# Sending each head's scores in two transfers, by two queues, with four banks for the first mixing

## The chip, the cores and the metric

The kernel runs on one core of a Trainium2 chip. The metric is device time of one execution in microseconds (us); the median of several executions is given for a kernel. Differences of about 1% are what a measurement of this kernel can tell from none. The engines are TensorE (PE in the rows; PEld is its loading of weights), VectorE (DVE), ScalarE (ACT), GpSimd (POOL) and SyncE (SP), which here only issues transfers.

## The reference

The reference is attention whose heads are mixed before and after the softmax, and then two layers of matrix products on its output. Only the attention is touched by the change.

```python
# q, k, v: (4 batches, 12 heads, 448 rows, 64); w_pre, w_post: (12, 12)
scores = scale * np.matmul(q, k.transpose(0, 1, 3, 2))
scores = np.einsum('bhij,hg->bgij', scores, w_pre)
scores = scores - np.max(scores, axis=-1, keepdims=True)
attn = np.exp(scores)
attn = attn / (np.sum(attn, axis=-1, keepdims=True) + 1e-09)
attn = np.einsum('bhij,hg->bgij', attn, w_post)
x = np.matmul(attn, v)                 # heads side by side: (1792, 768)
h = x @ w_in                           # (1792, 2048)
x = (h * np.cos(h)) @ w_out            # (1792, 768)
h = np.maximum(np.maximum(x @ w1, x @ w2), x @ w3)
return h @ w_out2
```

## The kernel before, in words

**Blocks, slots and visits.** The 448 score rows of a batch are cut into four blocks of 10, 12, 12 and 11 slots; a slot is ten rows (`RI`), so a block has 100 to 120 rows. There are 16 blocks, numbered through all batches. For a block, `qk` (L552) multiplies two heads at a time: four matmuls for each of the six pairs of heads, into a bank of PSUM for each head (pool `ps_x`, two banks). `evac` copies a head's scores to SBUF (tile `s`, on ScalarE or VectorE; the copy is recorded at L460), and `send` (L566) moves them by a transfer from SBUF to SBUF into the tile of slots, `t`. There a slot's ten rows of all twelve heads lie side by side on 120 partitions, so that heads can be mixed by a matmul. There are two tiles `t`, used by even and odd blocks in turn.

**A visit** takes two slots. `mix1` (L575) mixes the heads of both into two banks of the pool `ps_m` (half `a` of the rows in each), `rowmax` (L583, VectorE) and `soft` (L589, ScalarE, exp with the row sums) make the softmax of each bank into a tile `e`, the three small operations `guard` (L594), `recip` (L598) and `wscale` (L603) on VectorE make the second mixing's weights with the row sums in them (`w2s`), `mix2` (L616) mixes the heads again, which also transposes, into a bank of the pool `ps_t` for each slot, and `keep` copies the two banks to the tile `a2`. A batch has 23 visits.

**The product with v.** Two neighbouring blocks are one entry of `HALVES`; when all of its visits are kept, `av` (L640) multiplies by v in three pieces of two pairs of heads, each piece into two banks of `ps_t`, `keepx` copies them to `xs` (L460 again), and `out` (L655) sends them to DRAM (`xT`). Below, Q stands for the four matmuls of one `qk`, M for a visit's first mixing, X for its second, and A for a piece of `av`; Q6.5 is the last pair of heads of block 6, M6:0 the first visit of block 6, A3/1 the second piece of the fourth entry of `HALVES`.

**The layers behind.** xT is loaded a batch at a time into a place of the tiles `t` (`x<-xT`, L139) and cut in two parts; the weights are loaded (`wraw`), converted on ScalarE and VectorE, and the products run as matmuls at L156 to L158.

**What sets the order.** A planner (`Plan`) knows each operation's rank, what it comes after, the places that it takes and frees, and a duration for each engine that may do it, written in the code by hand (letters T, V, A, P and D for TensorE, VectorE, ScalarE, GpSimd and SyncE's queue). It picks one operation after another, and the engine for those that may run on two. Each engine then runs its own list in that fixed order, and waits where data are late. SP's transfers also run on eight semaphores in turn, so the ninth waits for the first to land.

## Time and profile before

| | |
|---|---|
| median of three runs | 1171.14 us (1169.19 to 1177.53) |
| the profiled execution's own time | 1172.04 us |
| its span from first to last instruction | 1170.3 us |
| TensorE busy | 1130.7 us, 97% of the span |
| VectorE busy | 992.9 us, 85% |
| ScalarE busy | 656.3 us, 56% |
| GpSimd busy | 79.8 us, 7% |

The shares are means over two stages. In the attention the matmuls are short and alternate between four kinds of work; in the layers behind they run without a gap. The profile gives a line's instructions in groups, the waits by who ended them, and the chain of work that ended last, in order of time.

### The profile page before, as it was taken

Reading aid. Unit: us, or ns where it says so; the run is one execution under the profiler, and the core shown is the slowest. Engines: PE = TensorE matmul, PEld = TensorE weight load, DVE = VectorE, ACT = ScalarE, POOL = GpSimd, SP = SyncE. Lnnn points to the kernel's source line nnn. Section 1 sums busy time; section 2 is a strip of 40 time slices with the busy share of each in tenths; the row PEclk is TensorE's granted clock in tenths of the full one; section 3 lists DMA queues with packets and bytes.
Section 4 is the critical chain, followed back from the end, with each engine's and each line's share of the span. In section 5 each row is a group of like instructions: output and inputs, shape, how many; then the busy total and the mean of one; then the engine's idle time right before and its main releaser. Section 6 shows DMA issues by size and latency. Waiting matters only on the chain.

```text
span 1170.3 us, 29431 instructions
## 1 busy us (share of the span) xinstructions
PE 1130.7 (97%) x11836; PEld 926.5 (79%) x11836; DVE 992.9 (85%) x2083; ACT 656.3 (56%) x1468; POOL 79.8 (7%) x69
## 2 busy tenths in 40 slices
PE   7899999899898899999999999999999999999998
PEld 2566566565556699999999999999999999999987
DVE  5878777777778899999999999997788679778994
ACT  3656556655657687555555555555534354445472
POOL 4000000000005110000000000000001021011110
PEclk9999999999999999999999999999999999999999
DMA  6785565645553655343434344431002221222233
GB/s 220 226 242 163 169 195 158 185 132 153 155 170 116 213 155 149 115 136 115 135 115 135 115 135 121 130 108 34 1 28 82 61 67 35 76 66 69 82 117 113
DMA packets 90696, 146.02 MB, mean 125 GB/s; under 512 B 8928, under 2 KB 73536, under 8 KB 90560
## 3 DMA queue, kind: packets, MB, share of 16 engines
q1 hardware_dynamic: 90304, 144.12, 40.8%
q8 instruction: 93, 1.52, 0.5%
q14 instruction: 43, 0.35, 0.1%
q0 software_dynamic: 256, 0.02, 0.0%
HBM read 84.96 MB, written 20.45 MB: 90 GB/s over the span
## 4 chain that ended last, share of the span: by engine, by line
PE 84%; DMA 6%; DVE 5%; issue 1%; ACT 1%; SPq 1%; ACTq 0%; DVEq 0%
PE ps L156 21%; PE ps L158 21%; PE ps L157 21%; PE mps L575 6%; PE aps L640 5%; PE aps L616 5%; PE ps L552 4%; DMA t<-s 3%; DMA x<-xT 1%; DVE nm L583 1%; DMA v<-in_v_dram 1%; DVE s L460 1%; DMA wraw<-in_w_in_dram 0%; ACT e L589 0%; DVE a L460 0%
## 5 line engine op out<-in xcount | busy, mean ns | idle before, releaser
L158 PE MATMUL ps<-x,w 128*128 128x448 f32 x816 | 300.0, 368 | 2.4 <-DVE x L147 1.5
L156 PE MATMUL ps<-x,w 128*128 128x448 f32 x816 | 300.4, 368 | 0.8 <-ACT gh L857 0.6
L157 PE MATMUL ps<-x,w 128*128 128x448 f32 x816 | 299.8, 367 | 0.5 <-DVE w L296 0.3
L156 PEld LDWEIGHTS ps<-x,w 128*128 128x128 f32 x816 | 153.7, 188 | 17.6 <-issue 2.4
L158 PEld LDWEIGHTS ps<-x,w 128*128 128x128 f32 x816 | 153.6, 188 | 17.4 <-POOL x L147 2.0
L157 PEld LDWEIGHTS ps<-x,w 128*128 128x128 f32 x816 | 153.7, 188 | 14.8 <-POOL w L131 0.8
L589 ACT ACTIVATE e<-mps,nm 128x448 f32<-128x448 f32 (+1 forms) x184 | 116.9, 637 | 79.2 <-DVE nm L583 59.3
L616 PEld LDWEIGHTS aps<-w2s,e 60*64 60x64 f32 x5760 | 108.7, 136 | 51.2 <-issue 23.8
L156 PE MATMUL ps<-gh,w 128*128 128x448 f32 x384 | 140.9, 367 | 0.0
L157 PE MATMUL ps<-gh,w 128*128 128x448 f32 x384 | 140.7, 366 | 0.0
L158 PE MATMUL ps<-gl,w 128*128 128x448 f32 x384 | 140.4, 366 | 0.0
L583 DVE TENSOR_REDUCE nm<-mps 128x1 f32<-128x448 f32 (+1 forms) x184 | 110.2, 616 | 30.8 <-PE mps L575 29.3
L293 ACT CAST w<-wf 128x384 fp32r<-128x384 f32 x168 | 81.1, 514 | 74.5 <-DVE wf L285 54.2
L616 PE MATMUL aps<-w2s,e 60*64 60x60 f32 x5760 | 112.7, 220 | 8.9 <-DVE w2s L603 6.2
L575 PE MATMUL mps<-t,w 64*64 64x448 f32 (+1 forms) x720 | 106.4, 558 | 10.2 <-DMA t<-s 6.2
L552 PE MATMUL ps<-k,q 64*64 64x448 f32 (+3 forms) x736 | 99.0, 551 | 5.1 <-ACT s L460 2.5
L814 DVE TENSOR_TENSOR acc<-ps,acc 128x448 f32<-128x448 f32 x168 | 100.2, 615 | 1.4 <-PE ps L158 1.4
L252 ACT ACTIVATE wf<-wraw 128x384 f32<-128x384 f32 x112 | 61.9, 553 | 51.3 <-DMA wraw<-in_w_out_dram 37.7
L296 DVE TENSOR_TENSOR w<-wf,w 128x384 fp32r<-128x384 f32 x132 | 73.7, 579 | 19.1 <-ACT w L293 18.3
L296 POOL TENSOR_TENSOR w<-wf,w 128x384 fp32r<-128x384 f32 x36 | 42.1, 1177 | 684.6 <-DVE wt L256 371.8
L640 PE MATMUL aps<-a,v 128*64 128x220 f32 (+1 forms) x768 | 78.0, 356 | 4.7 <-ACT xs L460 3.2
L640 PEld LDWEIGHTS aps<-a,v 128*64 128x64 f32 x768 | 54.2, 136 | 34.2 <-issue 5.9
(121 smaller groups left out, 1736.7 us busy)
## 6 DMA issues: line engine op xcount, KB each, us to landing
t<-s SPq DMA_DIRECT2D x96, 210.0 KB
wf<-w SPq DMA_DIRECT2D x96, 192.0 KB
wraw<-in_w_out_dram SPq DMA_DIRECT2D x44, 384.0 KB
wraw<-in_w_dram SPq DMA_DIRECT2D x36, 384.0 KB
wraw<-in_w_in_dram SPq DMA_DIRECT2D x32, 384.0 KB
t<-s SPq DMA_DIRECT2D x48, 192.5 KB
w<-wf SPq DMA_DIRECT2D x48, 192.0 KB
t<-s SPq DMA_DIRECT2D x43, 175.0 KB
```

The source lines that it names most:

```text
L156: mm(w[0], x[0], start=first, stop=False)
L157: mm(w[1], x[0], start=False, stop=False)
L158: mm(w[0], x[1], start=False, stop=last)
L293: return nc.scalar.copy(A[x][0], w())
L296: return eng.tensor_sub(A[x][1], w(), f32(A[x][0]))
L552: nc.tensor.matmul(live["s", n, 2 * hp + g][r:end], live["q", b, hp][half, i0 + r:i0 + end], live["k", b, hp][half], start=True, stop=True)
L575: nc.tensor.matmul(live["m", v, a][64 * y:64 * y + 64], w1[k], grids[n % 2][k, t + y, :], start=True, stop=True)
L583: nc.vector.tensor_reduce(nm, of(v, live["m", v, a]), axis=AX.X, op=ALU.max, negate=True)
L589: nc.scalar.activation(of(v, e), of(v, live["m", v, a]), AF.Exp, bias=live["nm", v, a], scale=1.0, accum_out=live["z", v][:, a:a + 1])
L616: nc.tensor.matmul(live["a", v, y][64 * c:64 * c + 64, j, :, a, :], live["e", v, a][k, o:o + 64], live["w2s", v][k, a], start=True, stop=True)
L640: nc.tensor.matmul(ps[64 * g:64 * g + 64, :m], vt[:, j, g, :], a2[:, j, 2 * hp + g, :m], start=j == 0, stop=j == JB - 1)
L814: return nc.vector.tensor_add(acc, po, acc) if fg else nc.scalar.copy(acc, po)
```

## The change

Four things change together.

- **Sends.** A head's scores of a block go in two transfers, one for slots 0 to 5 and one for the rest, and each is issued by SP or by GpSimd, as the planner finds. Each half of the tile `t` is a place of its own in the plan (`t0`, `t1`): a visit waits for the half that holds its slots, and a half is free once its visits are mixed. `keepx` copies in two parts for each block, since the rows are now spread over the slots of each half.
- **Banks.** `ps_m` has four banks instead of three and `ps_t` two instead of three; `av` puts both pairs of heads of a piece into one bank. `s` has seven tiles instead of eight, `e` six instead of five.
- **Blocks.** The first batch's first two blocks and the last batch's last two are entries of `HALVES` of their own, so there are ten entries and 30 pieces of `av` instead of 8 and 24. The last batch's blocks are in the order 12, 11, 12, 10.
- **The planner's numbers.** Durations and the times until a result can be used are written anew, and a piece of `av` stands behind a certain visit.

```diff
-HALVES = [[[10, 12], [12, 11]]] * B
+HALVES = [[[10], [12], [12, 11]], [[10, 12], [12, 11]], [[10, 12], [12, 11]], [[12, 11], [12], [10]]]
...
+HALF = 6
+BUFS = {"k": 10, "q": 9, "s": 7, "e": 6, "w2s": 3, "v": 7, "xs": 6, "a2": 2, "ps_m": 4, "ps_t": 2, "ps_x": 2}
...
-    def send(n, h, eng):
+    def send(n, h, y, eng):
         slots = score[n][3]
-        queue_of[eng].dma_start(grids[n % 2][PAD + h:PAD + RI * H:H, :slots, :], live.pop(("s", n, h))[:RI * slots])
+        start, end = y * HALF, min(slots, (y + 1) * HALF)
+        queue_of[eng].dma_start(grids[n % 2][PAD + h:PAD + RI * H:H, start:end, :],
+                                live["s", n, h][RI * start:RI * end])
...
-        for hp in pairs(x):
-            vt = live["v", b, hp]
-            live["av", hp] = ps_t.tile([128, JB, H, RI], F32, name="aps")
-            ps = live["av", hp] = live["av", hp].rearrange("p j g i -> p (j g i)")
+        both = ps_t.tile([128, JB * H * RI], F32, name="aps")
+        for n, hp in enumerate(pairs(x)):
+            ps = live["av", hp] = both[:, n * NHALF:(n + 1) * NHALF]
             for j in range(JB):
                 for g in range(2):
-                    nc.tensor.matmul(ps[64 * g:64 * g + 64, :m], vt[:, j, g, :], a2[:, j, 2 * hp + g, :m],
+                    nc.tensor.matmul(ps[64 * g:64 * g + 64, :m], live["v", b, hp][:, j, g, :], a2[:, j, 2 * hp + g, :m],
                                      start=j == 0, stop=j == JB - 1)
...
-            copy(eng, xs[:, o:o + m].rearrange("p (r t) -> p r t", t=slots),
-                 ps[:, c:c + m].rearrange("p (t r) -> p r t", r=RI))
+            for t in range(0, slots, HALF):
+                part, w = RI * t, min(HALF, slots - t)
+                copy(eng, xs[:, o + part:o + part + RI * w].rearrange("p (r t) -> p r t", t=w),
+                     ps[:, c + part:c + part + RI * w].rearrange("p (t r) -> p r t", r=RI))
...
-                add(evac, (n, h), r, {"A": 0.55, "V": 0.62}, [("qk", n, hp)], turn=True, takes=[place := copy_place(n, h)[0]], frees=[(ring, ("qk", n, hp), h % 2)])
-                if h == 0:
-                    plan.add(("new_t", n), r, lambda _: None, {}, [("evac", n, 0)], takes=["t"])
-                add(send, (n, h), r, {"D": score[n][2] / 118.0}, [("evac", n, h), ("new_t", n)], turn=True, frees=[(place, ("evac", n, h))], lands=2.5)
+                add(evac, (n, h), r, {"A": 0.42, "V": 0.53}, [("qk", n, hp)], turn=True, lands=0.16, takes=[place := copy_place(n, h)[0]], frees=[(ring, ("qk", n, hp), h % 2)])
+                for y in range(2):
+                    if h == 0:
+                        plan.add(("new_t", n, y), r, lambda _: None, {}, [("evac", n, 0)], takes=[f"t{y}"])
+                    add(send, (n, h, y), r + 0.2 * y, {"D": 0.78, "P": 0.78}, [("evac", n, h), ("new_t", n, y)],
+                        behind=[("send", n, h - 1, y)] if h else [], frees=[(place, ("evac", n, h))], lands=3.5)
...
-        add(mix1, (y,), i, {"T": 0.8}, [("wmix", 0), ("fill", n % 2)] + [("send", n, h) for h in range(H)], turn=True, takes=["ps_m"] * 2,
-            frees=[("t", ("new_t", n))])
+        add(mix1, (y,), i, {"T": 0.78}, [("wmix", 0), ("fill", n % 2)] + [("send", n, h, t // HALF) for h in range(H)], turn=True, takes=["ps_m"] * 2,
+            frees=[(f"t{t // HALF}", ("new_t", n, t // HALF))])
...
-        add(mix2, (y,), i + 1.5, {"T": 0.05 + 0.45 * len(slots)}, [key("wscale")], turn=True, takes=["ps_t"] * len(slots),
+        add(mix2, (y,), i + 1.5, {"T": 0.04 + 0.465 * len(slots)}, [key("wscale")], turn=True, takes=["ps_t"] * len(slots),
...
+    def from_visit(y):
+        return [("mix1", y)] if 0 <= y < len(visits) else []
...
+        room = min(12, starts[halves[half + 1][4][-1] + 1] - 1 - ylast) if half + 1 < len(halves) else 12
...
-            add(av, (half, x), r, {"T": 3.25}, [("vget", b, hp) for hp in pairs(x)] + ends, turn=True, takes=["ps_t"] * 2,
-                frees=[("a2", start)] + [("v", ("vget", b, hp)) for hp in pairs(x) if half % 2])
+            add(av, (half, x), r, {"T": 0.2 + 0.0139 * halves[half][3]}, [("vget", b, hp) for hp in pairs(x)] + ends, turn=True, takes=["ps_t"],
+                frees=[("a2", start)] + [("v", ("vget", b, hp)) for hp in pairs(x) if halves[half][1] + halves[half][2] == S],
+                behind=from_visit(ylast + 2 + x * room // 3))
...
-        add(xget, (n,), r, {"D": 3.6}, [("out", 2 * n + x, hp) for x in range(2) for hp in range(H // 2)] + [("xget", 0)] * n
-            + [("block", FG)], takes=["t"])
+        add(xget, (n,), r, {"D": 3.6}, [("out", x, hp) for x, y in enumerate(halves) if y[0] == n for hp in range(H // 2)] + [("xget", 0)] * n
+            + [("block", FG)], takes=["t0", "t1"])
...
-    plan.run({**BUFS, "t": 2, "ps": BUFS["ps_x"], "mark": NM, "u": 7,
+    plan.run({**BUFS, "t0": 2, "t1": 2, "ps": BUFS["ps_x"], "mark": NM, "u": 7,
```

How the order moves is shown at three places. In these rows `ps<-k,q` is Q (two rows for one), `mps<-t` is M, `aps<-w2s,e` is X, `aps<-a` is A, and `ps<-x,w` is the first product of the layers behind; a count behind a row is how often it stands there in sequence, so x8 at `mps<-t` is two visits and x64 at `aps<-w2s,e` two second mixings.

TensorE around the border between blocks 5 and 6, before: the first two rows are Q6.5, and the last but one is M6:0.

```order
L552 MATMUL ps<-k,q 64x448 x2
L552 MATMUL ps<-k,q 56x448 x2
L575 MATMUL mps<-t,w_124 64x448 x4
L616 MATMUL aps<-w2s,e 64x12x5 x32
L552 MATMUL ps<-k,q 64x448 x2
L552 MATMUL ps<-k,q 46x448 x2
L616 MATMUL aps<-w2s,e 64x12x5 x32
L575 MATMUL mps<-t,w_124 64x448 x4
L552 MATMUL ps<-k,q 64x448 x2
```

The same place in the changed kernel, again from Q6.5 on:

```order
L554 MATMUL ps<-k,q 64x448 x2
L554 MATMUL ps<-k,q 56x448 x2
L620 MATMUL aps<-w2s,e 64x12x5 x32
L554 MATMUL ps<-k,q 64x448 x2
L554 MATMUL ps<-k,q 46x448 x2
L620 MATMUL aps<-w2s,e 64x12x5 x32
L554 MATMUL ps<-k,q 64x448 x2
L554 MATMUL ps<-k,q 46x448 x2
L620 MATMUL aps<-w2s,e 64x12x5 x32
L579 MATMUL mps<-t,w_124 64x448 x8
L620 MATMUL aps<-w2s,e 64x12x5 x32
```

Between Q6.5 and M6:0 stood M5:5, X, Q, X; now X, Q, X, Q, X stand there, and M6:0 is followed at once by M6:1.

GpSimd's list from the loads of the mixing weights on, before: after the clearing of the tiles `t` it has nothing until the layers behind.

```order
L508 DMA wraw<-in_w_pre_dram 60x12 x2
L508 DMA wraw<-in_w_post_dram 60x12 x2
L506 DMA blk<-in_same_row_dram 60x10 x4
L498 MEMSET t 4x5376 x2
L147 ISA
```

GpSimd's list in the changed kernel, the same place (`10x6x448` is a half of six slots, `10x4x448` the other half of a block of ten):

```order
L508 DMA blk<-in_same_row_dram 60x10 x4
L500 MEMSET t 4x5376 x2
L569 DMA t<-s 10x4x448
L569 DMA t<-s 10x6x448
L569 DMA t<-s 10x4x448
L569 DMA t<-s 10x6x448
L569 DMA t<-s 10x4x448
L569 DMA t<-s 10x6x448
L569 DMA t<-s 10x4x448
L569 DMA t<-s 10x6x448 x26
```

In all, GpSimd issues 188 of the 384 half sends and SP 196; before, SP issued 192 whole ones.

TensorE from the last visit of block 14 (M14:5) to the first matmul of the layers behind, before:

```order
L575 MATMUL mps<-t,w_124 64x448 x4
L640 MATMUL aps<-a_5572,v_127 64x220 x8
L640 MATMUL aps<-a_5572,v_128 64x220 x8
L575 MATMUL mps<-t,w_124 64x448 x4
L616 MATMUL aps<-w2s,e 64x12x5 x32
L575 MATMUL mps<-t,w_124 64x448 x4
L616 MATMUL aps<-w2s,e 64x12x5 x32
L575 MATMUL mps<-t,w_124 64x448 x4
L616 MATMUL aps<-w2s,e 64x12x5 x64
L575 MATMUL mps<-t,w_124 64x448 x4
L156 MATMUL ps<-x,w 128x448
```

The same in the changed kernel, where the first row holds M14:4 and M14:5:

```order
L579 MATMUL mps<-t,w_124 64x448 x8
L620 MATMUL aps<-w2s,e 64x12x5 x32
L643 MATMUL aps<-a_5872,v_127 64x230 x8
L643 MATMUL aps<-a_5872,v_128 64x230 x8
L579 MATMUL mps<-t,w_124 64x448 x4
L620 MATMUL aps<-w2s,e 64x12x5 x64
L158 MATMUL ps<-x,w 128x448
```

One A, four Ms and four Xs stood between M14:5 and the first product; now one A, one M and three Xs do.

## Rows read from the trace of the kernel before

**Rows 1.** Busy time by stretch: PE, PEld, DVE, ACT, POOL, granted clock, DMA share, GB/s.

```profile
0.00:23.30 23.30, 16.26 (x84) 4.50 (x85) 12.29 (x22) 7.37 (x14) 13.56 (x14) 1.00 0.68 222
23.30:343.50 320.20, 303.07 (x7316) 187.00 (x7316) 250.04 (x658) 195.51 (x538) 0.00 (x0) 0.99 0.59 175
343.50:412.80 69.30, 58.82 (x757) 44.42 (x756) 61.10 (x124) 50.08 (x114) 22.66 (x19) 0.95 0.54 177
412.80:1170.30 757.50, 752.53 (x3683) 690.54 (x3681) 669.45 (x1280) 403.39 (x805) 43.57 (x38) 1.00 0.32 96
```

**Rows 2.** Waits in 23.3 to 343.5: TensorE idle; total us, times, longest.

```profile
PE mps L575 <- DMA t<-s: 6.2, 7, 1.6
...
PE mps L575 <- DMA q<-in_q_dram: 1.6, 1, 1.6
```

**Rows 3.** TensorE's timeline at the border of blocks 5 and 6: start, us, what.

```profile
134.62 0.95 PE L552 MATMUL ps<-k,q 64*64 64x448 f32 x8
135.37 1.58 PE L575 MATMUL mps<-t,w 64*64 64x448 f32 x5
...
140.00 1.16 PE L616 MATMUL aps<-w2s,e 60*64 60x60 f32 x64 [0.99 <-DVE w2s L603]
142.24 1.34 PE L575 MATMUL mps<-t,w 64*64 64x448 f32 x8 [1.08 <-DMA t<-s]
```

**Rows 4.** The chain that ended last, 104 to 146 us: start, us, what.

```profile
121.37 3.26 PE aps L640 x32
...
125.54 0.93 PE aps L616 x64
126.47 0.75 PE ps L552 x8
127.22 0.78 PE mps L575 x8
...
137.60 4.59 DMA t<-s
```

**Rows 5.** The same view, where block 0's last send is awaited.

```profile
20.09 3.17 DMA t<-s
```

**Rows 6.** Busy time and granted clock, as rows 1, just behind that border.

```profile
142.00:146.00 4.00, 3.76 (x61) 2.05 (x64) 1.78 (x3) 1.34 (x4) 0.00 (x0) 0.59 0.31 102
```

**Rows 7.** Waits of TensorE's weight loads in 23.3 to 343.5, as rows 2.

```profile
PEld mps L575 <- ACT e L589: 12.2, 20, 1.2
...
PEld aps L640 <- ACT a L460: 3.7, 5, 0.8
```

**Rows 8.** Groups by form in 23.3 to 343.5: count, busy us, mean ns, idle before.

```profile
L460 DVE COPY a<-aps 128x480 f32<-128x480 f32 x76 | 49.6, 653 | 8.3 <-PE aps L616 7.6
...
L460 DVE COPY xs<-aps 128x120 f32<-128x120 f32 x20 | 5.5, 277 | 8.0 <-PE aps L640 8.0
```

**Rows 9.** Weight loads of the product with v, whole run, columns as rows 8.

```profile
L640 PEld LDWEIGHTS aps<-a,v 128*64 128x64 f32 x768 | 54.2, 136 | 34.2 <-issue 5.9
```

**Rows 10.** SP's issues at L566, min/median/max ns; GpSimd's group; a GpSimd transfer's landing.

```profile
L566 SPq DMA_DIRECT2D t<-s x187: 755/756/1379, 7.2 to 338.1; - x187
...
L506 POOL DMA_DIRECT2D blk<-in_same_row_dram x4 | 2.1, 521 | 0.0
...
blk<-in_same_row_dram POOLq DMA_DIRECT2D x4, 2.3 KB, 5.2
```

**Rows 11.** The chain into the layers behind, as rows 4.

```profile
343.47 6.08 DMA x<-xT
```

**Rows 12.** Timeline of VectorE and GpSimd, 10 to 11 and 343 to 363 us.

```profile
10.46 4.19 DVE L514 TENSOR_SCALAR wraw<-wraw 128x12 f32<-128x12 f32 x1
...
343.06 0.28 DVE L603 TENSOR_TENSOR w2s<-w2t,rz 128x120 f32<-128x120 f32 x1
...
352.40 1.13 POOL L147 TENSOR_TENSOR x<-x 128x448 fp32r<-128x448 f32 x1 [337.78 <-DMA wraw<-in_w_in_dram]
...
352.89 0.78 DVE L603 TENSOR_TENSOR w2s<-w2t,rz 128x120 f32<-128x120 f32 x1
```

More of the change, by code (lines that the diff above doesn't have):

```diff
@@ L657, in attention, with add @@
     before = {}
-    def add(f, a, rank, engines, after=(), turn=False, **kw):
+    def add(f, a, rank, engines, after=(), turn=False, behind=(), **kw):
         key = f.__name__, *a
-        plan.add(key, rank, partial(f, *a), engines, after, behind=before.get(f, ()) if turn else (), **kw)
+        plan.add(key, rank, partial(f, *a), engines, after, behind=list(before.get(f, ()) if turn else ()) + list(behind), **kw)
         if turn:
@@ L666, in attention @@
     HP = H // 2
+    starts = [next(y for y, x in enumerate(visits) if x[0] == n) for n in range(NS)] + [len(visits)]
+    def from_visit(y):
+        return [("mix1", y)] if 0 <= y < len(visits) else []
     for x in range(3):
```

29 lines of the change are left out of this document (15 added, 14 removed).

## The prediction

> **What bounds the kernel now.** I read the busy time by stretch first [rows 1]. From 412.8 us on, TensorE is busy for 752.5 of 757.5 us: the layers behind the attention cannot get shorter by this change, and they start when the attention has handed over. So the whole question is how much earlier that is. Between the first visit at 23.3 us and the end of the last block but one at 343.5 us, TensorE is busy for 303.1 of 320.2 us, so 17.1 us of idle time are all that better waiting can give there directly; VectorE has 250.0, ScalarE 195.5 and GpSimd nothing. Behind it, up to 412.8, another 10.5 us are idle.
>
> The waits come next. 7.8 us of the 17.1 are a first mixing that waits for a send (6.2 under that name; 1.6 are put down to a load of q that ends beside the sends) [rows 2]. The timeline of one border between blocks shows how such a wait arises [rows 3]: the last Q of block 6 ends at 135.57 (134.62 + 0.95), its last send is issued at 137.60 and lands 4.59 us later [rows 4], and M6:0 starts at 142.24. That is 6.67 us, in which TensorE had one M, one Q and two Xs to do and then stood still, 0.99 us for the weights of a second mixing and 1.08 us for the send. The granted clock behind that pause is 0.59 on average from 142 to 146 us [rows 6], which is about 3.3 us at the lower of the two levels (1.2 instead of 2.4 GHz): some 1.7 us of delay.
>
> Idle time is not all. The M at 135.37 takes 1.58 us in two parts, where an undisturbed one takes 0.78 [rows 3, 4]: its second half had no bank. Weight loads of M waited 12.2 us in 20 cases for a softmax that held a bank, and those of A 3.7 us for a copy [rows 7]; this is hidden in TensorE's busy time.
>
> **The change, part by part**, against the profiled execution's own 1172.04 us. It lies 0.9 us above the median of the runs, so the result may be read against either.
>
> *Border waits.* For a border I need the time L from the end of the last Q to the landing of what M needs, and the work that stands between them. By the order, with 0.75 for Q, 0.78 for M, 0.93 for X and 3.26 for an A of 230 columns [rows 4], the changed kernel has 4.3 us of work there at two of the 15 borders (borders 1 and 6), 5.0 to 5.1 at four, 5.5 to 5.9 at seven, and over 9 at two. L was 6.67: 2.03 to the last issue and 4.64 from there to the start of M. Two queues can save up to one issue at the end, 0.756 [rows 10] and a little between, so 2.03 becomes 1.2 to 2.0; I take 1.4. A half has 60 instead of 120 rows; the landing lies between 4.59 and the 3.17 of a send when little else is on its way [rows 4, 5]; I take 3.9, the middle. With L = 5.3 the wait is 2 × 1.0 + 4 × 0.25 = 3.0 us instead of 7.8: −4.8. With L = 4.35 it is 0.1, with 6.67 it is 18.0: −7.7 to +10.2.
>
> *What follows from the pauses.* The slow stretch goes if the pause goes: −1.7 (−1.7 to 0). Of the other 9.3 us of idle time, some, as the 0.99 us above, come from a chain of visits that has run dry at a border; I take −2 (−9.3 to 0).
>
> *Four banks for M.* The 12.2 us of load waits are the most that this can give, and nothing the least, since part of such a wait lies beside the other half's matmuls. I take −6.
>
> *One bank for A instead of two.* −2 (−3.7 to 0) [rows 7]; the copies of the visits before it are still waited for where a piece is the first of its entry.
>
> *Two banks for X instead of three.* An X now needs both copies of the visit before. At 22 places of the changed order only one Q or one M, about 0.75 us, stands between two Xs. A copy takes 0.653 on VectorE [rows 8] and is just hidden if it starts at once; if its engine first finishes another one like it, 0.55 is left over, 12 us in all. I take a quarter, +3 (0 to +12).
>
> *Shorter pieces of A.* The columns are the same in all, but 12 of the 30 pieces have 100 or 120. By columns they take 1.45 and 1.74 us. If the loads bound them, it would be 54.2 / 24 = 2.26 us for each [rows 9]: 6 × 0.81 + 6 × 0.52 = 8.0. The short matmuls of X, with loads as long, run 32 in 0.93 us, so I lean to the columns: +2 (0 to +8).
>
> *Costed at nothing.* SP issues 196 half sends where it issued 192 whole ones; issues of 100 to 120 rows all take 0.756 us [rows 10], so its load stays, with 12 short stores more. GpSimd's 188 issues take 98 us at the 0.521 of its own transfers and 142 at SP's 0.756 [rows 10], in a stretch where it has no work [rows 1]; if that cover is gone, the third rival below follows. `keepx` makes 192 copies of at most 60 columns instead of 96; at 0.277 at most [rows 8] that is under 16 us more for each of ScalarE and VectorE, and eleven score copies move from VectorE to ScalarE; both have 70 us and more to spare [rows 1].
>
> *Start.* Up to the last first half of block 0, SP's list now has 16 sends instead of 12, 3 us more at 0.756, but the whole sends stood waiting for copies for about as long. The landing of the last one was 3.17 [rows 5]. I take 0 (−3 to +3).
>
> *Hand-over.* Between M14:5 and the first product stood 10.0 us of work, now 6.9, while the load of x that starts behind M14:5 takes over 6.08 us and must then be cut in two [rows 11]. That is 3 us more of waiting; against it, TensorE is idle for 10.5 us there anyway [rows 1] and part of it may go. +2 (−4 to +6).
>
> The sum: −4.8 − 1.7 − 2 − 6 − 2 + 3 + 2 + 0 + 2 = −9.5, so **1162 us**. The ends do not come together; taken as independent, they give the forecast 1154 to 1170.
>
> **The rivals.**
>
> *A: the sends stop counting.* If every half lands in 3.2 us, no border waits (−7.7), the slow stretch and half of the dry chains go (−1.7 and −5), and M, never late, gets 9 of its 12 us; with −2 for A, +1 for X, +1 for the short pieces and +1 for the hand-over this is −22: 1150. For it speaks that landings spread from 3.17 to 4.59 between a quiet moment and a busy one [rows 4, 5], with a mean busy share of 0.59 of the transfer engines [rows 1]; against it, that SP's half of the sends goes the same way as before. By the Trainium skill (DMA: Bandwidth & Descriptors, "Why a DMA increments its semaphore by 16 and not by 1") a send with ten rows of partitions as its outer size runs on ten of the sixteen engines, always the lowest ten from SP, but from GpSimd on ten that move round; that would lighten those ten. No row here shows which engines carry a send.
>
> *B: the wait stays.* If the landing keeps its length and GpSimd's sends land no sooner than SP's, L is about 6.0, the borders wait 2 × 1.7 + 4 × 0.95 + 7 × 0.3 = 9 us as before, and slow stretch and dry chains stay; −6 − 2 + 3 + 2 + 2 + 1.5 = 0.5: 1172. For it: a landing in the trace of a tiny GpSimd transfer took 5.2 us [rows 10].
>
> *C: GpSimd's issuing holds up VectorE.* A small VectorE operation that works in SBUF alone took 4.19 us while GpSimd cleared a tile, and a `wscale` 0.78 instead of 0.28 beside GpSimd's subtraction [rows 12]. If an issue does the same, each of a visit's three small operations meets one with a chance of 142 / 310 and waits half of 0.756: 0.17 us, 0.5 per visit, 45 us on VectorE for 86 visits. It is then busy for 295 of 310 us and the visits' chain is longer; TensorE pays about half, +22, and the kernel needs 1185. It decides from about 0.1 us per small operation, where half of 26 us eats the gain. Against it: an issue is not a sweep over a tile, and no row shows a delay by one. The Trainium skill (SBUF — State Buffer, "SBUF: two separate sides") says that VectorE in its two-port mode and GpSimd exclude each other for a whole instruction, and that GpSimd then cannot write its descriptors; the 4.19 us agree with the lock itself.
>
> **How the numbers follow.** Chances: forecast 0.50, A 0.15, B 0.22, C 0.13. About 1%, 12 us, is what a measurement of this kernel can tell from no change: below 1159 is faster, above 1183 slower. Faster: 0.22 of the forecast's 0.50 and nearly all of A, 0.36. Slower: most of C and a little of B, 0.14. Within 1%: 0.50. The range from 1149 to 1181 leaves out most of C, a third of A and the edges of the rest, 2 in 10.
>
> **What would show it.** After: the sends' waits of M in the attention at about 3 us (over 7 speaks for B, under 1 for A); the loads of M waiting for `soft` at half of 12.2 or less; X waiting for copies for a few us; pieces of A of 100 columns at 1.5 and not 2.3 us; GpSimd's issues at 0.5 to 0.8 us, and `guard` and `wscale` at their old lengths (longer ones are C); the first product's wait in the hand-over about 3 us longer. I am wrong altogether if GpSimd's issue takes over 1.65 us (310 / 188), since it then sets the pace itself, or if the two-bank pool makes every second X wait.

## The result, and the profile after

| | before | after |
| --- | --- | --- |
| median, us | 1170.16 (1166.53 to 1177.53, 10 runs) | 1180.36 (1177.16 to 1184.55, 10 runs) |
| profiled execution, and its span | 1172.04, 1170.3 | 1180.71, 1178.9 |
| ratio | | 1.0081 (95%: 1.0056 to 1.0105) |

The change makes the kernel slower by 0.8%, some 10 us. I forecast 1162, 8 us faster. The ratio is inside the 1% that I called no change, but its interval excludes both no change and my sign.

The same stretches as in [rows 1], cut at the first M of block 0, the first M of the last block and 757.5 us ahead of the end (busy us of TensorE, weight loads, VectorE, ScalarE, GpSimd, then granted clock, DMA share, GB/s):

```profile
0.00:26.60 26.60, 18.56 (x84) 4.96 (x85) 10.28 (x20) 8.34 (x15) 21.29 (x28) 0.84 0.73 215
26.60:356.50 329.90, 307.77 (x7322) 203.00 (x7322) 245.43 (x690) 202.66 (x586) 96.69 (x174) 0.97 0.62 173
356.50:421.40 64.90, 56.39 (x947) 45.12 (x946) 57.59 (x122) 50.84 (x132) 16.56 (x15) 1.00 0.53 170
421.40:1178.90 757.50, 752.53 (x3681) 690.24 (x3679) 670.40 (x1282) 404.15 (x807) 43.77 (x38) 1.00 0.32 96
```

Against [rows 1]: 3.3 us are lost before the first M, 9.7 in the attention (329.9 for 320.2), 4.4 are gained in the hand-over, and the layers behind take the same 757.5; the sum is +8.6, the difference of the spans. In the attention TensorE stands idle for 22.1 us instead of 17.1 and is busy 4.7 us longer at a lower mean clock.

The waits of TensorE, of its weight loads and of VectorE in that stretch answer to [rows 2, 7]:

```profile
PE mps L579 <- DMA t<-s: 6.2, 3, 3.4
PE ps L554 <- DVE s L462: 4.9, 2, 4.0
PE mps L579 <- DMA k<-in_k_dram: 3.3, 1, 3.3
...
PE mps L579 <- DMA q<-in_q_dram: 0.6, 1, 0.6
```

```profile
PEld aps L643 <- ACT a L462: 11.1, 15, 1.1
PEld aps L620 <- ACT a L462: 10.9, 19, 1.0
...
PEld mps L579 <- ACT e L593: 4.5, 10, 1.4
```

```profile
DVE s L462 <- DMA t<-s: 11.2, 4, 5.3
```

A first mixing reads only the slots in `t` and the mixing weights, so a wait of M for a transfer is a wait for a send, whatever name the profile gives to the landing (sends and loads share SP's eight semaphores); the prediction read the row on q so, and came to 7.8 us before. Read the same way, M now waits 10.1 us for sends, the most of it in three pauses of 2.0 to 3.4 us. The pause put down to a load of k shows it: M3:0 starts at 90.93 us, by the trace's semaphores that load lands only at 92.32, and a half send that SP issued at 83.86 had landed at 90.69. Two rows are new: a pause of 4.0 us in which a Q waits for VectorE's copy, and VectorE's copies of scores waiting 11.2 us in all for a send to give a place of s back. The weight loads of M wait less for a softmax (12.2 before), those of A more for a copy (3.7 before).

Where the first of the new waits comes from is seen on the timelines of GpSimd, VectorE, ScalarE and TensorE up to block 1 (start, us, what, idle time before it and what ended it):

```profile
5.64 9.08 POOL L500 MEMSET t<- 4x5376 f32 x2
14.68 2.80 POOL L569 DMA_DIRECT2D t<-s  x5
```

```profile
18.76 0.53 ACT L462 COPY s<-ps 120x448 f32<-120x448 f32 x1 [2.75 <-DMA t<-s]
```

```profile
19.34 1.75 PE L554 MATMUL ps<-k,q 64*64 64x448 f32 x2 [2.32 <-ACT s L462]
...
26.62 5.40 PE L579 MATMUL mps<-t,w 64*64 64x448 f32 x24 [0.77 <-DMA t<-s]
```

```profile
45.16 0.62 DVE L462 COPY s<-ps 120x448 f32<-120x448 f32 x1 [5.33 <-DMA t<-s]
```

GpSimd clears the two grids until 14.72 us, and its first five half sends stand behind that. Their places of s stay taken, ScalarE's copy waits 2.75 us for one, and TensorE stands still for 2.32. At 39.8 VectorE waits 5.33 us for a place, this time for a half that GpSimd issues at 38.67 us, long after the clearing, and that lands at 45.04. Block 1's first M begins at 49.01 (before: 38.70). The granted clock is 0.5 from 18.0 to 31.7 us; in the profile before it is full there.

The later pauses lie where loads come in between. Around the border of blocks 6 and 7, the busy times, the chain and TensorE's timeline show (the timeline's row is M7:0), and so do GpSimd's sends issued in this stretch (halves of six and of five slots: count, size, median us to landing):

```profile
166.00:178.00 12.00, 8.24 (x192) 5.33 (x188) 6.30 (x19) 6.23 (x20) 3.36 (x6) 1.00 0.93 227
```

```profile
170.75 7.07 DMA t<-s
```

```profile
177.80 1.21 PE L579 MATMUL mps<-t,w 64*64 64x448 f32 x8 [3.43 <-DMA t<-s]
```

```profile
t<-s POOLq DMA_DIRECT2D x4, 105.0 KB, 6.7
...
t<-s POOLq DMA_DIRECT2D x1, 87.5 KB, 7.6
```

The transfer engines are busy 0.93 of these 12 us. The send of 7.07 us that the chain names is a half of five slots, which M7:0 does not need; by the semaphores the last half that it needs was issued by SP at 169.88 and landed at 177.45, after 7.57 us, where I had reckoned with 3.9 and at most 4.59 [rows 4]. The loads of q and k issued between the sends take 5.7 to 7.8, and the sends of GpSimd take about as long as those of SP.

Taken over the whole attention, again by the semaphores (a transfer has landed with the last update before its queue uses that semaphore again), a half of six slots lands in 3.83 us from SP and 3.95 from GpSimd (medians). A whole send of twelve slots took 3.95 in the kernel before and takes 4.19 in the one with whole sends below, so half the rows bring 0.4 us at most.

### The profile page after: what moved, and what is told of

Same layout as the page of the kernel before. It is cut to its first block, busy times and chain, and to the rows that moved or that the text cites. A ratio compares the mean times of both kernels' runs of the same rounds, so it can differ in the third digit from the quotient of the medians.

```text
span 1178.9 us, 30512 instructions
## 1 busy us (share of the span) xinstructions
PE 1135.3 (96%) x12028; PEld 943.3 (80%) x12028; DVE 983.7 (83%) x2112; ACT 666.0 (56%) x1538; POOL 178.3 (15%) x254
## 4 chain that ended last, share of the span: by engine, by line
PE 82%; DMA 6%; DVE 5%; issue 3%; ACT 2%; POOL 2%; SPq 0%; DVEq 0%; POOLq 0%; ACTq 0%
PE ps L158 21%; PE ps L159 21%; PE ps L160 21%; PE mps L579 5%; PE aps L620 5%; PE aps L643 4%; PE ps L554 4%; DMA t<-s 3%; DMA x<-xT 1%; POOL t L569 1%; DVE nm L587 1%; POOL t L500 1%; DMA k<-in_k_dram 0%; DVE x L335 0%; DVE a L462 0%
## 5 line engine op out<-in xcount | busy, mean ns | idle before, releaser
L620 PEld LDWEIGHTS aps<-w2s,e 60*64 60x64 f32 x5760 | 119.2, 137 | 47.1 <-issue 21.0
L569 POOL DMA_DIRECT2D t<-s x188 | 104.4, 557 | 226.9 <-ACT s L462 115.9
L620 PE MATMUL aps<-w2s,e 60*64 60x60 f32 x5760 | 121.5, 222 | 8.2 <-DVE xs L462 2.8
L587 DVE TENSOR_REDUCE nm<-mps 128x1 f32<-128x448 f32 (+1 forms) x184 | 107.2, 614 | 25.5 <-PE mps L579 24.8
L554 PE MATMUL ps<-k,q 64*64 64x448 f32 (+3 forms) x736 | 107.1, 571 | 9.4 <-DVE s L462 4.9
L579 PE MATMUL mps<-t,w 64*64 64x448 f32 (+1 forms) x720 | 94.9, 569 | 11.7 <-DMA t<-s 6.2
L643 PEld LDWEIGHTS aps<-a,v 128*64 128x64 f32 x960 | 58.2, 136 | 31.2 <-ACT a L462 11.8
```

The lines of the kernel that those rows point to most:

```text
L554: nc.tensor.matmul(live["s", n, 2 * hp + g][r:end], live["q", b, hp][half, i0 + r:i0 + end], live["k", b, hp][half], start=True, stop=True)
L569: queue_of[eng].dma_start(grids[n % 2][PAD + h:PAD + RI * H:H, start:end, :], live["s", n, h][RI * start:RI * end])
L579: nc.tensor.matmul(live["m", v, a][64 * y:64 * y + 64], w1[k], grids[n % 2][k, t + y, :], start=True, stop=True)
L587: nc.vector.tensor_reduce(nm, of(v, live["m", v, a]), axis=AX.X, op=ALU.max, negate=True)
L620: nc.tensor.matmul(live["a", v, y][64 * c:64 * c + 64, j, :, a, :], live["e", v, a][k, o:o + 64], live["w2s", v][k, a], start=True, stop=True)
L643: nc.tensor.matmul(ps[64 * g:64 * g + 64, :m], live["v", b, hp][:, j, g, :], a2[:, j, 2 * hp + g, :m], start=j == 0, stop=j == JB - 1)
```

## The experiments

Ratios are to the kernel before, run beside each group (medians 1169.5 to 1170.5), with their 95% interval. To see where a kernel wins or loses, I read the start of the first row maximum of a block on VectorE's timeline, in its profiled execution:

| us | block 1 | block 4 | block 12 | blocks 4 to 12 | last X or A | span |
| --- | --- | --- | --- | --- | --- | --- |
| before | 39.7 | 99.4 | 277.0 | 177.6 | 388.0 | 1170.3 |
| after | 50.0 | 113.6 | 291.5 | 177.9 | 395.6 | 1178.9 |
| clear late | 43.1 | 107.4 | 281.1 | 173.7 | 385.3 | 1170.2 |
| whole sends | 46.9 | 107.9 | 275.3 | 167.4 | 377.7 | 1161.9 |
| split in before | 46.5 | 111.6 | 280.9 | 169.3 | 385.7 | 1166.8 |
| split, old order | 53.0 | 114.8 | 288.7 | 173.9 | 391.1 | 1172.5 |
| whole, old order | 45.3 | 115.5 | 290.8 | 175.3 | 395.5 | 1176.4 |
| split, no q, k loads | 46.2 | 104.3 | 268.2 | 163.9 | 371.3 | 1153.7 |
| whole, no q, k loads | 45.4 | 97.4 | 261.9 | 164.5 | 364.2 | 1146.8 |
| whole, scores twice | 42.3 | 104.1 | 269.0 | 164.9 | 370.9 | 1155.3 |
| split, scores twice | 51.2 | 114.6 | 287.9 | 173.3 | 391.5 | 1177.6 |

One thing limits most of these comparisons. Each edit is planned anew, and the planner then changes TensorE's list also far from the edited place. Between Q7.5 and M7:0 the changed kernel has one M, one A, one Q and one X, 5.7 us of work by the prediction's prices; with whole sends two Ms, two As, two Qs and three Xs stand there, 12.4 us, and a late landing is hidden. A difference between two kernels is that of the edit together with its order. The list stays nearly as it was in the kernels with the late clearing and with the scores computed twice, and, among those with whole sends, where loads of q and k go by GpSimd or are left out.

**Four kernels on the first reading.** GpSimd's second clearing after block 0's sends:

```
-        add(fill, (n,), -60.0, {"P": 5.0})
+        add(fill, (n,), -60.0, {"P": 5.0}, [("send", 0, h, y) for h in range(H) for y in range(2)] * n)
```

> The second tile of slots is cleared by GpSimd only after all of block 0's half sends are issued; nothing else is changed. Theory 1 (the start: half sends of block 0 stand in GpSimd's list behind its two clearings until 14.7 us, their tiles s come free late, TensorE pauses, and the granted clock falls from 18 to 31.6 us): GpSimd's first half send is issued at about 10.2 us, the stretch at the lower clock level goes, the first visit starts at 22 to 23.5 us instead of 26.6, block 1 at 39 to 41 instead of 49.0, and the kernel takes 1170 to 1173 us. Rival (the start is late because SP's half sends are twice as many, or because a tile s is held by two landings): the first visit stays at 26 or later and the time at 1178 to 1181.

1174.58, ratio 1.0046 (1.0025 to 1.0066). GpSimd's first send goes out at 10.16 instead of 14.68, VectorE's long wait for a place is gone, and M1:0 starts 6.9 us earlier:

```profile
42.11 1.73 PE L579 MATMUL mps<-t,w 64*64 64x448 f32 x16 [0.38 <-DMA t<-s]
```

About half of what the change loses comes back from this one edit, 6.2 us at the start and 4.2 in blocks 4 to 12. What I expected of the clock did not come: it is still at half from 20 to 24 us, and the time is above the 1170 to 1173 that went with it.

One more place for s, one less for e:

```
-"s": 7, "e": 6
+"s": 8, "e": 5
```

> Eight tiles s and five e as before the change, instead of seven and six; nothing else. Theory 3 (a tile s is held until both halves have landed, so copies of scores wait for a place: 11.2 us on VectorE and 2.4 on ScalarE in the changed kernel, one of them the 3.95 us pause at border 1): these waits fall to under 5 us and the kernel takes 1173 to 1177. Rival (places of s are not what holds the copies, or five tiles e cost as much): 1178 to 1183.

1185.05, ratio 1.0149 (1.0116 to 1.0182): slower by 5 us, though VectorE's waits for a place of s fall from 11.2 to 0.7 us. In its profile block 1 starts at 46.8 and block 4 at 109.3 (50.0 and 113.6 in the changed kernel), so the place for s helps at the start; blocks 4 to 12 then take 184.2 us instead of 177.9. Whether the place taken from e or the other order loses that was not separated.

The split undone, all else in the code kept (new banks, blocks, places, table of times):

```
-HALF = 6
+HALF = RT
-                for y in range(2):
+                for y in range(1):
-  {"D": 0.78, "P": 0.78}
+  {"D": 0.78}
```

> The split is undone and all else kept: whole sends by SP alone, one place for the tile of slots, keepx in one copy for each block; four banks for M, two for X and A, the new entries of HALVES and the planner's new numbers stay. Theory 1 (the split costs: the start, and the pauses over 3 us at borders): block 1 starts at about 39 us as before the change and the kernel takes 1160 to 1167. Rival (banks, blocks or the new order cost it): 1176 to 1182, with the loads of X and A waiting for copies as long as in the changed kernel (about 15 and 10 us).

1162.40, ratio 0.9926 (0.9904 to 0.9948). With the order that the planner makes for it, the split costs 18 us here, and the rest of the change gains 8. Block 1 does not start near 39 us, as expected, but at 46.9. The attention's row and TensorE's waits (same cuts as above):

```profile
25.20:338.50 313.30, 297.04 (x7320) 198.87 (x7320) 237.38 (x640) 202.90 (x556) 0.00 (x0) 0.98 0.62 181
```

```profile
PE mps L579 <- DMA k<-in_k_dram: 5.5, 2, 4.7
...
PE mps L579 <- DMA t<-s: 4.3, 3, 2.0
```

M's wait for whole sends, with 0.8 us for those sent from a tile `e`, is 10.6 us, as long as for the halves. Of the 16.6 us between the two attentions (329.9 and 313.3), 5.9 are idle time of TensorE and 10.7 lie in its busy time, for as many matmuls (7322 and 7320) at a mean clock of 0.97 and 0.98. So the greater part of the split's cost shows in no wait of TensorE. The same DMA share of 0.62 moves 181 GB/s instead of 173: over all transfers of the stretch a byte keeps the transfer engines 4.6% longer with half sends (181 / 173).

No loads of q and k for batches 1 to 3:

```
+        if b:
+            live["k", b, hp] = live["k", 0, hp]
+            return
```

> Leaves out the loads of q and k for batches 1 to 3 (36 of 48 loads; batch 0's tiles are used again, so the output of batches 1 to 3 is another). Theory 2 (the long landings of 6.5 to 7.6 us at borders 3, 7 and 9 come from those loads, which land beside the last sends of a batch): the waits of 3.3 us at border 3 and 3.4 at border 7 and the slow clock behind them go, last landings are 3 to 5 us there, and the kernel takes 1168 to 1171, with the start as late as in the changed kernel. Rival (the two halves of a send slow each other, whatever else is on its way): landings of 6 us and more stay at two or three borders and the time at 1176 or more.

1156.31, ratio 0.9901 (0.9867 to 0.9935), 24 us below the changed kernel and well below the 1168 to 1171 expected. These loads meet the sends somewhere; a second run below shows how much of it is the split's.

**Which queue.** All half sends by GpSimd, then all by SP:

```
-  {"D": 0.78, "P": 0.78}
+  {"P": 0.56}      (the second: {"D": 0.78})
```

> As the changed kernel (1180.4), but GpSimd issues all 384 half sends, SP none. Theory T1 (it is the number of transfers: twice as many, each landing as late as a whole one, crowd the loads of q and k and hold the places of s, whoever issues them): within 1174 to 1187, landings near 3.7, waits for sends, k and s together again near 14 us. Theory T2 (it is SP's list: sends of SP wait for copies and keep the loads of q, k and the second halves behind them): SP is now free, the loads go early, 1162 to 1172, and the wait for k disappears. Against both at the start: GpSimd's first send comes after its clearings at 14.7 us, which may add 3 us.

1181.55, ratio 1.0088 (1.0063 to 1.0114), as the changed kernel. Block 4 starts 3 us later (116.8), behind GpSimd's clearing, and blocks 4 to 12 take 4 us less (173.8): SP's list, freed of every send, explains little. The landing hardly improves either (issues of this kernel: count, size, median us to landing; the same row has 3.7 in the changed kernel):

```profile
t<-s POOLq DMA_DIRECT2D x282, 105.0 KB, 3.6
```

> As the changed kernel, but SP issues all 384 half sends at 0.75 us, GpSimd none. 24 sends are 18 us of issuing in a block of about 20.5 us, beside loads. T1: SP becomes the bound at the borders too, 1190 to 1215. If it were GpSimd's issuing that costs (by whatever way), this kernel would be near the whole sends' 1162 to 1172.

1231.39, ratio 1.0519 (1.0491 to 1.0548), above the range given. SP issues 384 halves at 0.749, 288 us in a stretch of some 330, and loads stand behind them:

```profile
PE ps L554 <- ACT s L462: 11.6, 11, 3.5
PE ps L554 <- DMA k<-in_k_dram: 10.1, 8, 2.6
```

Nothing here speaks for GpSimd's issuing as the cost, and on SP's queue alone the split costs far more than it can bring. In this slower kernel, with the transfer engines busy 0.50 of the time from 23.3 to 390 us, a half of six slots lands in 2.7 us (median, by the semaphores).

**The split alone**, put into the kernel before (three banks, old order, places and table; `send`, `keepx` and the rows on `t0`, `t1` as in the change):

> The kernel before (1170.2) with the split alone: two half sends by SP or GpSimd and the pieces of the copies of x, but three banks for M, three for A, the old order of the blocks, the old places (s 8, e 5) and the old table of times. T1: the split costs by itself, near 18 us as in the changed kernel, so 1182 to 1192. T3 (the split only costs together with the new banks, order and places): 1166 to 1175. What I predicted of the split alone (waits at borders 4.8 less, what follows them 3.7 less): 1162.

1172.09, ratio 1.0019 (1.0000 to 1.0039): 0 to 5 us, not 18. The first mixings' waits for sends fall about as I had forecast (3.0 left), from 7.8 to 2.4 us:

```profile
PE mps L578 <- DMA t<-s: 2.4, 4, 1.3
```

In the table it loses 12.2 us by block 4 and gains 8.3 in blocks 4 to 12 (177.6 to 169.3). So there the split, with the list made for it, gains at the later blocks and pays it back at the start.

**Better queues for whole sends.** The loads of q and k by GpSimd, then this with the late clearing as well:

```
-  add(qget, (b, hp), r - early, {"D": 0.6}, ...
+  add(qget, (b, hp), r - early, {"P": 0.6} if b else {"D": 0.6}, ...   (kget too)
```

> As the kernel with whole sends (1162.4, whose longest wait in the attention is 4.7 us for a load of k), with the loads of q and k of batches 1 to 3 issued by GpSimd, which has nothing else to do there, in place of SP. If these loads are late because they stand behind sends that wait for copies on SP: 1153 to 1159, and no wait for k. If they are late because their places in k and q come free late: 1160 to 1165, the wait for k stays.

1163.17, ratio 0.9948 (0.9921 to 0.9974): the time stays. The rows on k are gone, and a longer one on a load of v has come:

```profile
PE mps L579 <- DMA v<-in_v_dram: 6.3, 1, 6.3
```

This is no wait for v. It ends at 27.18 us with M0:0, and by the semaphores a send of block 0, issued at 16.70 on the semaphore that SP next gives to a load of v, landed at 27.05. So in neither of the two kernels does a first mixing wait for a load, and the question was put wrongly.

> The best parts so far put together: whole sends (1162.4), the second grid cleared only after block 0's sends, the loads of q and k of later batches by GpSimd. If GpSimd's clearing delays the start without split sends too (VectorE's small step beside it took 3.3 us): 1156 to 1160. If it only hurt because GpSimd's sends stood behind it: 1160 to 1166, as the whole sends with loads by GpSimd (1163.2).

1166.21, ratio 0.9972 (0.9947 to 0.9996). No gain; the loss of 3 against the run before is not clear, since the intervals overlap. Where no sends stand behind it on GpSimd, the clearing costs no time that these runs show.

**The kernel before once more**, for its clock:

> The kernel before once more, for a second profile. In the first one TensorE's granted clock was full from the start to 142 us; in every changed kernel so far it fell to half at 17 to 22 us for 10 to 17 us, and at the border of block 4 before's first profile is 7 to 17 us ahead of theirs. If the fall at the start belongs to the change, this profile shows full clock up to 40 us again and block 1 near 39.7; if it is chance or belongs to the start of any of these kernels, a half-clock stretch begins near 17 us and block 1 starts near 45.

1171.60 in its one run. Block 1 starts at 39.8, and the clock is full until 234.6 us. The busy times from 12 to 40 us of this second execution, of the changed kernel and of whole sends, one row each in this order:

```profile
12.00:40.00 28.00, 22.45 (x401) 10.15 (x397) 18.30 (x43) 15.43 (x38) 2.61 (x1) 1.00 0.64 208
```

```profile
12.00:40.00 28.00, 22.32 (x307) 8.90 (x299) 14.57 (x36) 14.74 (x38) 13.71 (x21) 0.76 0.74 200
```

```profile
12.00:40.00 28.00, 23.65 (x357) 10.26 (x357) 16.34 (x41) 14.09 (x36) 2.62 (x1) 0.76 0.65 192
```

Neither profile of the kernel before has the fall, and changed kernels have it with the split or without; TensorE is as busy as before, but gets through 307 or 357 matmuls instead of 401.

**Which part of the rest makes the split dear.** The old cutting of the blocks, with the split and with whole sends; and three banks each:

```
-HALVES = [[[10], [12], [12, 11]], [[10, 12], [12, 11]], [[10, 12], [12, 11]], [[12, 11], [12], [10]]]
+HALVES = [[[10, 12], [12, 11]]] * B
```

> The changed kernel (1180.4) with the old cutting of the blocks into halves of a batch (10, 12 | 12, 11 in each batch). The split alone cost 2 us, the rest alone gained 8, both together lose 10: some part of the rest makes the split dear. If it is the new order of blocks: 1163 to 1172. If it is not: 1176 to 1185.

1173.64, ratio 1.0041 (1.0021 to 1.0060), between the two ranges.

> Whole sends (1162.4) with the old cutting of the blocks into halves of a batch. With the split the old order gave back 7 us (1173.6). If the new order makes the split dear (first half of 10 rows alone, its pieces of A and outputs inside the first blocks): the old order is no gain here, or a loss, 1165 to 1172, and the split costs only 2 to 8 in the old order, as in the kernel before. If the order is better or worse by itself, whatever the sends: 1153 to 1158.

1174.79, ratio 1.0047 (1.0022 to 1.0072): a loss, and a larger one than the first theory gave. So in the old order the split costs nothing (1173.6 against 1174.8), in the new order 18 us; and the new order gains 12 us with whole sends and loses 7 with halves. M's waits for sends in these two kernels (23.3 to 345 us, all names), halves first:

```profile
PE mps L579 <- DMA t<-s: 1.5, 3, 0.7
...
PE mps L579 <- DMA q<-in_q_dram: 1.4, 1, 1.4
```

```profile
PE mps L579 <- DMA t<-s: 13.4, 4, 8.6
...
PE mps L579 <- DMA xT<-xs: 3.8, 2, 2.6
PE mps L579 <- DMA v<-in_v_dram: 1.5, 1, 1.5
PE mps L579 <- DMA q<-in_q_dram: 1.1, 1, 1.1
```

With the old order M waits 19.8 us for whole sends and 2.9 for halves, with the new one 10.6 and 10.1. In the old order the split takes 17 us of waits away, and the time falls by 1; in the new order it takes none away, and the time grows by 18. M's waits for sends are real, but they do not add up to the time.

```
-"ps_m": 4, "ps_t": 2
+"ps_m": 3, "ps_t": 3
```

> The changed kernel with three banks for M and three for X and A, as before (A's pairs still share a bank). If the fourth bank of M or the missing third of X makes the split dear (scores and mixing crowd each other, X waits for copies 21 us): 1163 to 1173. If the banks have nothing to do with it, this loses their gain too: 1182 to 1192.

1186.61, ratio 1.0136 (1.0114 to 1.0159): the banks are not to blame; four for M and two for the rest, with their order, are worth 6 us.

**What the loads have to do with it.** Whole sends without the loads of q and k:

> Whole sends without the loads of q and k for batches 1 to 3 (their output is another). With the split, leaving them out gave back 24 us (1156.3). If the split is dear because its many transfers and these loads delay each other: whole sends gain little without them, 1155 to 1161, and without the loads the split costs nothing. If the split costs by itself and the loads cost by themselves: 1162.4 - 24 = 1138 to 1144.

1149.03, ratio 0.9825 (0.9783 to 0.9867), between the two theories. Without the loads the split costs 7 us (1156.3 against 1149.0), with them 18. The table splits this by place: without the loads blocks 4 to 12 take 163.9 us with halves and 164.5 with whole sends, no difference; with them 177.9 and 167.4. What is left without the loads, 6.9 us, is lost before block 4 (104.3 against 97.4).

**The start.** Old order and late clearing together:

> The changed kernel with the old order of blocks (1173.6 alone) and the second grid cleared after block 0's sends (1174.6 alone). If the two repair different stretches: 1180.4 - 6.8 - 5.8 = 1168, 1165 to 1171, level with before. If both repair the same stretch at the start: 1172 to 1176.

1173.26, ratio 1.0026 (1.0008 to 1.0044): the two do not add up. They do not repair the same stretch at the start either. In the old order block 4 starts no earlier than in the changed kernel (114.8), and with the late clearing too it starts at 114.5; the gain lies in blocks 4 to 12, which take 173.9 and here 171.0 us.

The scores of six pairs of heads at the start computed twice, with whole sends and with the split:

```
-        for r in range(0, m, 64):
+        for r in list(range(0, m, 64)) * (2 if 3 <= HP * n + hp < 9 else 1):
```

> Whole sends (1162.4), with the scores of six pairs of heads at the start (from the fourth pair of block 0 to the third of block 1) computed twice into the same bank, so that TensorE works in pauses it has there anyway. If the clock falls because of TensorE's pauses at 14 to 17 us: full clock up to 40 us, block 1 starts 3 to 6 us earlier, 1155 to 1161. If it falls for another reason, or because TensorE does more: the stretch stays, TensorE does more at half clock, 1163 to 1168.

In the profile the clock is full up to 64 us and M1:0 starts at 41.30 instead of 45.07:

```profile
16.31 2.32 PE L554 MATMUL ps<-k,q 64*64 64x448 f32 x16 [0.64 <-ACT s L462]
...
41.30 1.73 PE L579 MATMUL mps<-t,w 64*64 64x448 f32 x16 [1.38 <-DMA t<-s]
```

So more work in TensorE's pauses kept the clock up, in that execution. The time is 1160.39, ratio 0.9920 (0.9891 to 0.9948), 2 us under whole sends alone with overlapping intervals: the gain of the profile is not established over the runs.

> The changed kernel (1180.4) with the scores of six pairs of heads at the start computed twice, as in the kernel with whole sends (there the clock stayed full, block 1 started 4.6 us earlier, and the time was 1160.4 against 1162.4). If the split's cost is mostly the start at half clock: 1168 to 1174. If it is at the later borders: 1175 to 1179.

1183.05, ratio 1.0103 (1.0086 to 1.0121), above both ranges. The clock is full from 12 to 28 us, and block 1 is no earlier (51.2), since TensorE stands at 42 us for the same place of s as in the changed kernel:

```profile
46.23 1.00 PE L554 MATMUL ps<-k,q 64*64 64x448 f32 x3 [4.27 <-DVE s L462]
```

The half clock at 18 us is not what the split costs at the start (two later stretches at half clock, from 28 and from 45 us, stay). What holds TensorE here is the place for s; with eight of them, under another list, block 1 started at 46.8.

**Second halves later.** From block 1 on, a second half only after the first half of the head three further on:

```
-behind=[("send", n, h - 1, y)] if h else []
+behind=([("send", n, h - 1, y)] if h else []) + [("send", n, min(h + 3, H - 1), 0)] * (y and n)
```

> The changed kernel (1180.4), from block 1 on with each head's second half sent only after the first half of the head three further on. If the first halves are late because the second halves stand between them: the last first halves land 2 to 3 us sooner at the late borders, 1168 to 1175. If the engines are full anyway, with loads and whatever else, or because the places of s are now held longer: 1178 to 1190, with more waits of copies for a place of s.

1194.21, ratio 1.0205 (1.0185 to 1.0226), more than the range allowed. M waits 7.2 us for sends instead of 10.1, so the first halves are indeed awaited less, but the copies' waits for a place on VectorE and on ScalarE grow:

```profile
DVE s L462 <- DMA t<-s: 12.2, 7, 7.6
```

```profile
ACT s L462 <- DMA t<-s: 13.7, 11, 3.1
```

ScalarE waited 2.4 us for this in the changed kernel. A send cut in two holds its place until the later half has landed; delaying that half, with the order that follows, costs 14 us.

## Why the prediction was wrong

**The steps that failed are "Start" and "Border waits".**

*Start: 0 (−3 to +3).* I counted SP's list and the last landing, and did not look at what stands ahead on the second queue. Measured: M0:0 is 3.3 us late (1.9 with whole sends), and block 4 starts 14.2 us later than before (113.6 for 99.4). By the table 8.5 of it are there with whole sends too, and 5.7 come with the split. The split's part is GpSimd's sends behind its own clearing and the places of s that these hold: starting the sends first, with nearly the same list, brings block 4 forward by 6.2. Of the 8.5, the profile with scores computed twice gets 3.8 back at full clock; the rest I did not separate.

*Border waits: −4.8 (−7.7 to +10.2).* Measured, by the same reading: 10.1 us for 7.8, so +2.3. The range held this sign, the value did not. The work that I had counted at the borders stands there, but for two of the four borders at 5.0 to 5.1 us, which have 4.7, since their M is a visit of one slot. What was wrong is the landing. I took one whole send's 4.59 as the price of twelve slots and let a half land in 3.9 because it has half the rows. Over the attention a half does take 3.83 to 3.95, but a whole send took no more than 3.95 before; and at the two borders with the longest waits it takes 6.83 (M3:0) and 7.57 (M7:0), where the transfer engines are busy 0.89 and 0.93 of the 12 us around. In the kernel before, the split alone (with the list made for it) does take 5.4 us of such waits away. I also added the term to a new order that by itself, with whole sends, brings such waits from 19.8 to 10.6 us; two remedies for one wait don't add up. *What follows from the pauses*, −3.7, went the other way with it: the mean granted clock of the attention is 0.97 instead of 0.99.

These waits are the smaller part, though. The terms on banks were to shorten TensorE's busy time in the attention; it is 4.7 us longer than before, at the lower clock, and 10.7 longer than with whole sends. No term of the sum has a price for that.

Together, by the table, the 17 us of span that the split and its order cost are 5.7 up to block 4, 10.5 in blocks 4 to 12, none of it in the kernels without the loads of q and k, 1.7 in the last batch and 0.9 less behind it.

One sum of the prediction does not come out as written. The ends of the terms, taken as independent (root of the summed squares), lie 13 below and 20 above the forecast, 1150 to 1183 and not 1154 to 1170. The measured 1180.4 lies at the edge of the stated range, but by nothing that the range was drawn from; that is luck.

**What held.** Four banks for M, −6, and two for X, +3: the waits of M's loads for a softmax fell from 12.2 to 4.5, under the half I asked for, X's loads wait 10.9 us for copies, and three banks each lose 6.2 us, a net −6 where the two terms have −3. Short pieces of A take what their columns say, in the chain 1.53 for 100 columns (1.45 forecast, 2.26 the other bound):

```profile
50.74 1.53 PE aps L643 x32
```

*Hand-over*, +2 (−4 to +6), came out at −4.4, just outside, although the load of x took 7.62 instead of 6.08 [rows 11]. *One bank for A*, −2, has the wrong sign by its row, 11.1 us of load waits for copies instead of 3.7; what that costs was not measured apart.

**The rivals.** C is out. GpSimd's issues are as short as I took them at the lower bound, and VectorE's small operations keep their length beside them (groups by form: count, busy us, mean ns; [rows 12] has 0.28 for the second):

```profile
L569 POOL DMA_DIRECT2D t<-s x188 | 104.4, 557 | 226.9 <-ACT s L462 115.9 <-DVE s L462 36.1 <-DVE rz L602 26.4
```

```profile
L607 DVE TENSOR_TENSOR w2s<-w2t,rz 128x120 f32<-128x120 f32 x88 | 24.4, 277 | 1.3
```

A, sends that stop counting, is out by the landings. B, the wait that stays, named the right outcome at the borders (9 us of waits, 10.1 measured), at 1172; it lacked the start and the longer busy time. By the number C lies nearest, at 1185, which is luck, as its mechanism is absent. None of the three ended slower for the reason that did it.

**Open.** What makes TensorE's busy time longer with the split, and how much of the 18 us is the split's and how much that of the planner's other list: no run keeps the list and changes the sends alone. Why the granted clock falls at 17 to 22 us in most changed kernels and in neither profile of before: TensorE was not clearly less busy ahead of it (with whole sends 2.82 of the 4 us from 12 to 16, before 1.83). And which feature of the new order makes the kernel with whole sends so much faster: the table only places the gain, about equally up to block 4 (107.9 with whole sends against 115.5 in the old order) and in blocks 4 to 12 (167.4 against 175.3), and the middle batches are cut alike in both.

The best version measured keeps the banks, the new order, the places and the table, and sends each head whole by SP: 1162.4, 0.7% under before and 1.5% under the changed kernel. Computing some scores twice on top gives 1160.4, no different within the error.

## What to carry to other kernels

Do not count on half a transfer landing sooner: here it clearly did only in the one kernel whose transfer engines had the most time to spare (2.7 us at a busy share of 0.50; at 0.62 some 3.9, and a whole one 4.19). Read their busy share in the stretch where the transfer is awaited, not its mean. The source's place stays taken until the later part has landed, and a second queue brings with it whatever stands on it already, here 9 us of clearing. Gains that remove the same wait (an order that starts sends earlier, a send that lands earlier) are to be priced with each other in place, not added. And where a planner writes the order, compare the lists before a difference is put down to the edit.

## What the runs showed of the hardware

Around M7:0, with the transfer engines busy 0.93 of 12 us, everything issued from 165.9 to 175 us, half sends, loads of q and k and small stores, lands after 5.7 to 7.8 us, on either queue. Over the attention, at a mean share of 0.62, a half of six slots takes 3.83 us from SP and 3.95 from GpSimd, counted from the start of the issue; a whole send of twelve slots takes 4.19 at the same share and took 3.95 before, at 0.59. GpSimd issues a half send in 0.557 us beside 0.749 for SP's, and VectorE's small operations keep their length beside it; what GpSimd's sends wait for is the other work on that engine and the copies that they send. A landing that the profile names behind a wait can be another transfer on the same semaphore: the load of k named for M3:0 landed 1.4 us after M3:0 had begun.

The Trainium skill (DMA: Bandwidth & Descriptors, "Why a DMA increments its semaphore by 16 and not by 1") puts SP's sends with an outer size of ten on the ten lowest of the sixteen transfer engines, and GpSimd's, as a rule, on ten that move round, which I had weighed as a help for rival A. The trace agrees as far as the number on SP goes: a send's semaphore is updated eleven times, once early and then by ten landings. The median landing with every send on GpSimd, 3.6 us beside 3.7, shows no gain of the kind that rival A needs; which engines carried a send, no row shows.
